# First layer of two 512-token chunks by seven block products (Strassen's scheme) in a last part of its own

## The chip, the cores and the metric

The kernel runs on one core of a Trainium2 chip. The metric is device time in microseconds (us) of one execution. Engines are named as in the profile: PE is TensorE (PEld its weight loads), DVE is VectorE, ACT is ScalarE, POOL is GpSimd, SP is SyncE, which here only issues loads.

## The reference

Four batches, 8 heads, 576 positions of 64 numbers go through an attention of two parts (one on means of four neighbours, one in a band of 7 positions); their sum is x, 2304 tokens of 512 numbers. Then follows a mixture of 8 experts in which every token goes through every expert:

```python
for e in range(E):                      # E = 8
    h = np.maximum(x @ w1[e], 0.0)      # [2304, 512] @ [512, 1024]
    ye = h @ w2[e]                      # [2304, 1024] @ [1024, 512]
    out += P[:, e:e + 1] * ye
```

P (2304 x 8) is the gate: exp of x @ w_gate, normalized by rows and columns in turn, eight times. It is known only when all of x is.

## The kernel before

The tokens are cut into chunks: 0, 1 and 5 have 256 tokens (small), 2, 3 and 4 have 512. F = 1024 is cut into eight blocks of 128, f = 0 to 7. Every fp32 operand is split into a high part in a 32-bit matmul type and a low part (operand minus high part), and a product is made of three matmuls: high by high, high by low, low by high.

A unit is one (expert, f): a w1 block and a w2 block of 256 KB each. `w_load` (L172, L175) loads them on SP's queue into the pool rawp, three units deep; `w_convert` has ACT copy the high part (L193) and POOL subtract the low part (L200; a few on DVE, L203). A step is one unit for one chunk. `mm1` (L957) makes h transposed: 4 blocks of the 512 inputs by 3 matmuls, 12 in all, with the weights stationary and up to 512 tokens moving, into a PSUM bank. ACT's relu gives the high part hh (L963), DVE's instruction from the bank and hh the low part hl (L966). `mm2` (L976 to L978) makes ye: 3 matmuls of 512 columns for each tile of 128 tokens, accumulated over the eight f. `mm1` of the next step stands ahead of `mm2` of this one.

Phase A runs while attention is still being computed. Its passes are in the list `order`: chunk 0 for e = 0 to 3, chunks 0 and 1 together for e = 4 to 7, then chunk 2, then chunk 3, for all e. There is no gate yet, so each pass's ye goes to DRAM (`spill`, L1145). Phase A ends at the first pass boundary behind which the gate is known. A planner with estimated costs (`pump`) mixes the attention's instructions in.

Phase B goes through the experts once; for each it takes chunk 3, chunk 4, chunk 1 (for e = 0 to 3) and chunk 5, so a unit is used by three or four steps. Units with f = 0 to 3 go to the pool wa, those with f = 4 to 7 to the pool wb, on the other (right) side of SBUF. `combine` (L1198, L1203) adds P times ye to the accumulator of a tile; `back_load` and `back_add` bring the spilled tiles back, up to three at a time, one add a step. Tiles that are complete go out by ACT's queue (L1209).

The order of instructions on each engine is that of the program.

## Time and profile before

| | |
|---|---|
| time, median of 3 | 1734.27 us (1733.5 to 1735.94) |
| profiled execution | 1733.57 us, span 1731.8 us |
| PE, PEld busy | 98%, 81% |
| DVE, ACT, POOL busy | 45%, 29%, 39% |
| PE clock granted, mean | 0.988 of full speed |
| DMA | 178.12 MB, mean 103 GB/s |

The span is the time from the first to the last instruction. Busy time is a share of the span; matmuls overlap, so PE's pace is read from the starts of its matmuls.

### The profile page before, as it was taken

What the parts mean: (1) busy time and instruction counts of PE and PEld (TensorE: products, weight loads), DVE (VectorE), ACT (ScalarE), POOL (GpSimd) and SP (SyncE); (2) the same over time, 40 slices, a digit from 0 to 9 for tenths busy, and PEclk for the clock granted to TensorE, in tenths of its full rate; (3) what the DMA queues carried; (4) which work ended last, traced back from release to release, by engine and by line L of the source; (5) the groups of instructions that cost most, each with busy time, mean ns of one, the idle gap of its engine ahead of it and who ended that gap; (6) DMA issues with size and microseconds to landing.
All of it is one profiled execution on the core that took longest, in us unless ns stands there. A gap on an engine that the chain in (4) does not pass through costs nothing.

```text
span 1731.8 us, 21860 instructions
## 1 busy us (share of the span) xinstructions
PE 1691.7 (98%) x8457; PEld 1405.0 (81%) x8457; DVE 787.0 (45%) x922; ACT 494.8 (29%) x1030; POOL 676.9 (39%) x479
## 2 busy tenths in 40 slices
PE   6988999999999999999999999999999999999998
PEld 4877888788788877888888888888888888888887
DVE  7678887798788784513433421121111111211112
ACT  1554443444344333331121131131131221311210
POOL 5889886587676554440040040040040220401300
PEclk7899999999999999999999999999999999999999
DMA  8786666677577533341251240030030120300101
GB/s 200 197 235 190 170 186 178 169 192 183 154 168 183 138 116 116 115 137 47 73 183 49 67 134 1 0 98 1 0 110 1 37 62 1 97 1 13 49 25 37
DMA packets 177609, 178.12 MB, mean 103 GB/s; under 512 B 10850, under 2 KB 127088, under 8 KB 177506
## 3 DMA queue, kind: packets, MB, share of 16 engines
q1 hardware_dynamic: 166754, 157.33, 34.2%
q10 hardware_dynamic: 10752, 19.40, 3.2%
q8 instruction: 66, 1.08, 0.3%
q14 instruction: 37, 0.30, 0.1%
HBM read 157.29 MB, written 19.40 MB: 102 GB/s over the span
## 4 chain that ended last, share of the span: by engine, by line
PE 78%; issue 10%; POOL 5%; DMA 5%; DVE 2%; ACT 0%; SPq 0%; POOLq 0%; ACTq 0%; DVEq 0%
PE psh L957 38%; PE psy L976 13%; PE psy L978 12%; PE psy L977 12%; DMA r<-in_moe_w_dram 3%; POOL w1l L200 2%; POOL w2l L200 2%; DVE lo L367 1%; POOL dr L449 1%; DMA dr<-in_k_dram 1%; DMA dr<-in_v_dram 1%; PE pss L673 0%; PE psg L808 0%; DMA lq<-in_q_dram 0%; PE psx L771 0%
## 5 line engine op out<-in xcount | busy, mean ns | idle before, releaser
L200 POOL TENSOR_TENSOR w1l<-r,w1h 128x512 fp32r<-128x512 f32 x192 | 280.3, 1460 | 867.6 <-ACT w1h L193 842.7
L966 DVE SCALAR_TENSOR_TENSOR hl<-psh,hh 128x512 fp32r<-128x512 f32 (+1 forms) x352 | 208.5, 592 | 851.7 <-ACT hh L963 851.6
L957 PE MATMUL psh<-xh,w1h 128*128 128x512 f32 (+1 forms) x1408 | 502.7, 357 | 2.7 <-ACT w1h L193 2.1
L957 PE MATMUL psh<-xl,w1h 128*128 128x512 f32 (+1 forms) x1408 | 497.6, 353 | 3.8 <-POOL xl L792 2.0
L957 PE MATMUL psh<-xh,w1l 128*128 128x512 f32 (+1 forms) x1408 | 497.4, 353 | 1.2 <-POOL w1l L200 1.2
L963 ACT ACTIVATE hh<-psh 128x512 fp32r<-128x512 f32 (+1 forms) x352 | 182.7, 519 | 981.2 <-PE psh L957 962.7
L976 PE MATMUL psy<-w2h,hh 128*128 128x512 f32 x1152 | 456.6, 396 | 0.1
L978 PE MATMUL psy<-w2h,hl 128*128 128x512 f32 x1152 | 451.8, 392 | 0.0
L977 PE MATMUL psy<-w2l,hh 128*128 128x512 f32 x1152 | 451.8, 392 | 0.0
L957 PEld LDWEIGHTS psh<-xh,w1h 128*128 128x128 f32 x1408 | 266.9, 190 | 47.0 <-ACT w1h L193 2.5
L957 PEld LDWEIGHTS psh<-xl,w1h 128*128 128x128 f32 x1408 | 267.2, 190 | 45.9 <-DVE xl L795 2.7
L957 PEld LDWEIGHTS psh<-xh,w1l 128*128 128x128 f32 x1408 | 267.1, 190 | 39.2 <-POOL w1l L200 1.8
L200 POOL TENSOR_TENSOR w2l<-r,w2h 128x512 fp32r<-128x512 f32 x183 | 272.5, 1489 | 42.5 <-ACT w2h L193 41.1
L978 PEld LDWEIGHTS psy<-w2h,hl 128*128 128x128 f32 x1152 | 216.4, 188 | 48.6 <-DVE hl L966 0.2
L976 PEld LDWEIGHTS psy<-w2h,hh 128*128 128x128 f32 x1152 | 216.9, 188 | 42.1 <-ACT hh L963 0.3
L977 PEld LDWEIGHTS psy<-w2l,hh 128*128 128x128 f32 x1152 | 216.8, 188 | 41.2
L193 ACT ACTIVATE w2h<-r 128x512 fp32r<-128x512 f32 x192 | 121.1, 630 | 166.1 <-POOL w1l L200 54.6
L367 DVE TENSOR_REDUCE lo<-prod 128x256 f32<-128x1792 f32 x36 | 123.8, 3441 | 0.3
L193 ACT ACTIVATE w1h<-r 128x512 fp32r<-128x512 f32 x192 | 120.1, 625 | 12.4 <-ACT sp L1144 6.0
L274 DVE TENSOR_TENSOR prod<-lq,lw 128x1792 f32<-128x1792 f32 x34 | 81.6, 2400 | 4.4 <-DMA lw<-in_k_dram 3.9
L336 DVE TENSOR_TENSOR prod<-lw,sc 128x1792 f32<-128x1792 f32 x33 | 79.4, 2405 | 0.6
L297 DVE TENSOR_REDUCE sc<-prod 128x28 f32<-128x1792 f32 x36 | 72.2, 2009 | 2.0 <-POOL prod L274 1.8
(121 smaller groups left out, 673.9 us busy)
## 6 DMA issues: line engine op xcount, KB each, us to landing
r<-in_moe_w_dram SPq DMA_DIRECT2D x384, 256.0 KB
spill<-sp ACTq DMA_DIRECT2D x56, 256.0 KB
s<-spill SPq DMA_DIRECT2D x56, 256.0 KB
dr<-in_k_dram SPq DMA_DIRECT2D x32, 144.0 KB
dr<-in_v_dram SPq DMA_DIRECT2D x32, 144.0 KB
dr<-in_q_dram SPq DMA_DIRECT2D x24, 144.0 KB
out_dram<-acc ACTq DMA_DIRECT2D x12, 256.0 KB
lw<-in_v_dram SPq DMA_DIRECT2D x4, 640.0 KB
```

Source lines behind the costliest of these rows:

```text
L193: nc.scalar.activation(out=h, in_=r, func=AF.Copy)
L200: nc.gpsimd.tensor_tensor(out=l, in0=r, in1=h.bitcast(F32), op=ALU.subtract)
L274: eng.tensor_tensor(out=pr[:, r0:r0 + nr], in0=with_free(qt[:, h, r0:], [(D, nr), (0, W), (1, D)]), in1=with_free(kt[:, h, r0:], [(D, nr), ...
L297: nc.vector.tensor_reduce(out=sc[:, h, r0:r0 + nr], in_=pr[:, r0:r0 + nr], axis=AX.X, op=ALU.add)
L336: eng.tensor_tensor(out=pr[:, r0:r0 + nr], in0=with_free(vt[:, h, r0:], [(D, nr), (D, W), (1, D)]), in1=with_free(sc[:, h, r0:], [(W, nr), ...
L367: nc.vector.tensor_reduce(out=ot[:, r0:r0 + nr, h % 2], in_=pr[:, r0:r0 + nr].rearrange("p r w d -> p r d w"), axis=AX.X, op=ALU.add,)
L957: nc.tensor.matmul(out=ps, lhsT=w[:, kk], rhs=x[:, kk], start=(i == 0), stop=(i == len(seq) - 1))
L963: nc.scalar.activation(out=hh, in_=ps, func=AF.Relu)
L966: nc.vector.scalar_tensor_tensor(out=hl, in0=ps, scalar=0.0, in1=hh.bitcast(F32), op0=ALU.max, op1=ALU.subtract)
L976: nc.tensor.matmul(out=y, lhsT=hh[:, ts], rhs=h2, start=(f == 0), stop=False)
L977: nc.tensor.matmul(out=y, lhsT=hh[:, ts], rhs=l2, start=False, stop=False)
L978: nc.tensor.matmul(out=y, lhsT=hl[:, ts], rhs=h2, start=False, stop=(f == NF - 1))
```

## The change

Chunks 3 and 4 leave the common passes. In front of them, everything else is finished: `order` now ends with chunks 1 and 5 together for e = 0 to 3 (their x lies side by side in the tiles xhs and xls) and chunk 5 for e = 4 to 7. There is one pass for one set of units there, so each step has a unit of its own, all in wa. In these steps two spilled tiles are added a step, and `t_gen` makes the four sums and differences T1 to T4 of the blocks of x of chunks 3 and 4 (high and low part), into the new pool cx.

The last part goes through experts and halves of F. A half has four f. `w1_gen` takes two raw blocks of w1 and makes high and low parts of A11, A12, A22 and of the sums S1 to S4 for a pair of f, into wb for the first pair and wa for the second; it runs during the second layer of the half before. `m_pair` makes h of two f and two chunks by seven products of 256 x 128 x 512 with six matmuls each, and puts them together in PSUM (two products are added onto a bank that has been read) and by ACT and DVE. The high and low parts of h of a whole half lie in tiles that earlier held x of the small chunks (chunk 3) and of chunk 2 (chunk 4). Then the second layer of the half follows for 8 tiles, with a `combine` for each tile and half.

Also, the pool su4 goes: the first chunk's `xs` and `qf` use the h buffers of the pool hp. Pool accp closes before the last part, and accumulators and intermediate tiles of the last part (accc, ct) take its place.

```diff
--- before.py
+++ after.py
+    smalls = [c for c in range(NC) if is_small(c)]
+    NS = R * chunks[0][1]
+    for nm in ("xhs", "xls"):
+        x01.append(xp.tile([128, KD, len(smalls) * NS], F32R, name=nm))
+    for i, c in enumerate(smalls):
+        xh[c], xl[c] = (x[:, :, i * NS:(i + 1) * NS] for x in x01)
...
-        xs = (ap2 if c else su4).tile([128, R, n], F32, tag="xs", name="xs")
+        pl, tg = (ap2, "xs") if c else (hp, ("hh", "hl")[p // 2])
+        xs = pl.tile([128, R, n], F32, tag=tg, name="xs")
...
-        qf = ini.tile([128, 2, 2, 2, Q0], F32, name="qf")
+        qf = hp.tile([128, 2, 2, 2, Q0], F32, tag="hl", name="qf")
         nc.vector.memset(qf, 0.0)
 
         n_small = 4
         order = [((0,), e) for e in range(n_small)] + [((0, 1), e) for e in range(n_small, E)]
-        order += [((c,), e) for c in (2, 3) for e in range(E)]
-        late = {}
+        order += [((2,), e) for e in range(E)]
+        order += [((1, NC - 1), e) for e in range(n_small)] + [((NC - 1,), e) for e in range(n_small, E)]
...
+        ca, cb = 3, 4
+        n_done = n // NF
+        rest = order[n_done:]
...
+        cx = ctx.enter_context(tc.tile_pool(name="cx", bufs=1, side="right"))
         wb = ctx.enter_context(tc.tile_pool(name="wb", bufs=4, side="right", reuse_waits="tile"))
+        th4 = cx.tile([128, 2 * KD, NS * 2], F32R, name="th4")
+        tl4 = cx.tile([128, 2 * KD, NS * 2], F32R, name="tl4")
+        few = ExitStack()
+        accp = few.enter_context(tc.tile_pool(name="accp", bufs=1, side="right", reuse_waits="tile"))
+        spr = few.enter_context(tc.tile_pool(name="spr", bufs=3, side="right", reuse_waits="tile"))
...
+        def t_gen():
+            for kk in range(2):
+                b11, b12, b21, b22 = (
+                    wb.tile([128, DM], F32R, tag="w1h" if kk == 0 else "w1l", name="bsum").bitcast(F32)
+                    for _ in range(4)
+                )
+                for b, c, k0 in ((b12, cb, 0), (b11, ca, 0), (b22, cb, 2), (b21, ca, 2)):
+                    nc.vector.tensor_tensor(
+                        out=b, in0=xh[c][:, k0 + kk].bitcast(F32), in1=xl[c][:, k0 + kk].bitcast(F32), op=ALU.add
+                    )
+                    yield
+
+                nc.vector.tensor_tensor(out=b11, in0=b12, in1=b11, op=ALU.subtract)
+                yield
+                nc.vector.tensor_tensor(out=b12, in0=b22, in1=b12, op=ALU.subtract)
+                yield
+                nc.vector.tensor_tensor(out=b22, in0=b22, in1=b11, op=ALU.subtract)
+                yield
+                nc.vector.tensor_tensor(out=b21, in0=b22, in1=b21, op=ALU.subtract)
...
+                for i, b in ((0, b11), (1, b22), (2, b12), (3, b21)):
+                    nc.scalar.activation(out=th4[:, 2 * i + kk], in_=b, func=AF.Copy)
+                    nc.vector.tensor_tensor(
+                        out=tl4[:, 2 * i + kk], in0=b, in1=th4[:, 2 * i + kk].bitcast(F32), op=ALU.subtract
+                    )
...
+        def w1_gen(pl, dst):
+            ra, rb = c_raw.pop(0), c_raw.pop(0)
+            hs = [pl.tile([128, KD, 128], F32R, tag="w1h", name="c1h") for _ in range(4)]
+            ls = [pl.tile([128, KD, 128], F32R, tag="w1l", name="c1l") for _ in range(4)]
+            dst.append((hs, ls))
+            top, bot = slice(0, 2), slice(2, 4)
+            def hi(i, r, s=slice(0, 4)):
+                nc.scalar.activation(out=hs[i][:, s], in_=r[:, s], func=AF.Copy)
+            def lo(i, r, s=slice(0, 4)):
+                nc.gpsimd.tensor_tensor(
+                    out=ls[i][:, s], in0=r[:, s], in1=hs[i][:, s].bitcast(F32), op=ALU.subtract
+                )
+            def tt(o, a, b, op):
+                nc.gpsimd.tensor_tensor(out=o, in0=a, in1=b, op=op)
+            hi(0, ra)
+            hi(1, rb, bot)
+            yield
+            lo(0, ra)
+            lo(1, rb, bot)
+            tt(rb[:, bot], rb[:, top], rb[:, bot], ALU.add)
+            tt(rb[:, top], ra[:, top], rb[:, top], ALU.subtract)
+            tt(ra[:, top], rb[:, bot], ra[:, top], ALU.subtract)
+            tt(ra[:, bot], ra[:, bot], ra[:, top], ALU.subtract)
+            yield
+            hi(2, ra)
+            hi(3, rb)
+            yield
+            lo(2, ra)
+            lo(3, rb)
+            for _ in range(2):
+                c_load()
+            yield
...
+        def w2_conv(f):
+            r = c_raw.pop(0)
+            h2 = wa.tile([128, DM], F32R, tag="w2h", name="w2h")
+            l2 = wa.tile([128, DM], F32R, tag="w2l", name="w2l")
+            nc.scalar.activation(out=h2, in_=r, func=AF.Copy)
+            nc.gpsimd.tensor_tensor(out=l2, in0=r, in1=h2.bitcast(F32), op=ALU.subtract)
+            w2_ops[f] = h2, l2
+            c_load()
...
+        for i, (piece, e) in enumerate(rest):
+            for f in range(NF):
+                steps.append((piece, e, f, n_a + i * NF + f))
...
+            while n_cv[0] < min(n + 5, len(units)):
                 w_convert(t2)
...
+                for _ in range(2):
+                    back_load()
+                    back_load()
+                    back_add()
+                next(tg, None)
+                next(tg, None)
+            if n_cv[0] >= len(units) and len(c_raw) >= 2:
+                if g0 is None:
+                    g0 = w1_gen(wb, wq)
+                next(g0, None)
...
+        few.close()
...
+        hh_of = {ca: x01[0][:, :, 0:512], cb: xh[2]}
+        hl_of = {ca: x01[1][:, :, 0:512], cb: xl[2]}
+        top, bot = slice(0, 2), slice(2, 4)
+        x_op = {
+            "B11": (xh[ca][:, top], xl[ca][:, top]),
+            "B21": (xh[ca][:, bot], xl[ca][:, bot]),
+            "B22": (xh[cb][:, bot], xl[cb][:, bot]),
+        }
+        for i in range(4):
+            s = slice(2 * i, 2 * i + 2)
+            x_op[f"T{i + 1}"] = th4[:, s], tl4[:, s]
+        w_op = {
+            "A11": (0, top), "A12": (0, bot), "A22": (1, bot),
+            "S2": (2, top), "S4": (2, bot), "S3": (3, top), "S1": (3, bot),
+        }
...
+        def bank():
+            pl, tag = ((ps_h, "h"), (ps_a, "a"))[bank_n[0] % 2]
+            bank_n[0] += 1
+            return pl.tile([128, DM], F32, tag=tag, name="psm")
+        def prod(ps, a, b, w, start=True):
+            i, s = w_op[a]
+            wh, wl = w[0][i][:, s], w[1][i][:, s]
+            bh, bl = x_op[b]
+            seq = [z for kk in range(2) for z in ((wh, bh, kk), (wh, bl, kk), (wl, bh, kk))]
+            for j, (wt, xt, kk) in enumerate(seq):
+                nc.tensor.matmul(
+                    out=ps, lhsT=wt[:, kk], rhs=xt[:, kk], start=start and j == 0, stop=j == len(seq) - 1,
+                    skip_group_check=not start,
+                )
+        def relu(c, f, t):
+            nc.scalar.activation(out=hh_of[c][:, f], in_=t, func=AF.Relu)
+        def relu_lo(c, f, t):
+            nc.vector.scalar_tensor_tensor(
+                out=hl_of[c][:, f], in0=t, scalar=0.0, in1=hh_of[c][:, f].bitcast(F32),
+                op0=ALU.max, op1=ALU.subtract,
+            )
...
+        def m_pair(w, f1, between):
+            f2 = f1 + 1
+            pa1 = bank()
+            prod(pa1, "A11", "B11", w)
+            s1 = ctile()
+            nc.scalar.activation(out=s1, in_=pa1, func=AF.Copy)
+            pb = bank()
+            prod(pb, "A12", "B21", w)
+            c11 = htile("hh")
+            nc.vector.tensor_tensor(out=c11, in0=pb, in1=s1, op=ALU.add)
+            relu(ca, f1, c11)
+            prod(pa1, "S2", "T2", w, start=False)
+            u2 = ctile()
+            nc.scalar.activation(out=u2, in_=pa1, func=AF.Copy)
+            relu_lo(ca, f1, c11)
+            between()
+            pd = bank()
+            prod(pd, "S3", "T3", w)
+            u3 = ctile()
+            nc.vector.tensor_tensor(out=u3, in0=pd, in1=u2, op=ALU.add)
+            pg = bank()
+            prod(pg, "S1", "T1", w)
+            c22 = htile("hl")
+            nc.vector.tensor_tensor(out=c22, in0=pg, in1=u3, op=ALU.add)
+            relu(cb, f2, c22)
+            relu_lo(cb, f2, c22)
+            ph = bank()
+            prod(ph, "A22", "T4", w)
+            c21 = htile("hh")
+            nc.vector.tensor_tensor(out=c21, in0=u3, in1=ph, op=ALU.subtract)
+            relu(ca, f2, c21)
+            relu_lo(ca, f2, c21)
+            between()
+            prod(pg, "S4", "B22", w, start=False)
+            c12 = htile("hl")
+            nc.vector.tensor_tensor(out=c12, in0=pg, in1=u2, op=ALU.add)
+            relu(cb, f1, c12)
+            relu_lo(cb, f1, c12)
+        def y_mm(y, c, t, f):
+            hh, hl = hh_of[c], hl_of[c]
+            h2, l2 = w2_ops[f]
+            ts = slice(t * 128, (t + 1) * 128)
+            nc.tensor.matmul(out=y, lhsT=hh[:, f, ts], rhs=h2, start=(f == 0), stop=False)
+            nc.tensor.matmul(out=y, lhsT=hh[:, f, ts], rhs=l2, start=False, stop=False)
+            nc.tensor.matmul(out=y, lhsT=hl[:, f, ts], rhs=h2, start=False, stop=(f == 3))
...
+                m_pair(wq[0], 0, between)
+                for g in gens:
+                    for _ in g:
+                        pass
+                m_pair(wq[1], 2, w2_next)
+                del wq[0:2]
+                for f in conv:
+                    w2_conv(f)
...
+                gens = []
+                if not last:
+                    gens = [w1_gen(wb, wq), w1_gen(wa, wq)]
+                def w1_next():
+                    for g in gens[:1]:
+                        if next(g, 0) == 0:
+                            del gens[0]
+                yt = [ps_y.tile([128, DM], F32, tag="y", name="psy") for _ in range(4)]
+                for f in range(2):
+                    for t in range(4):
+                        y_mm(yt[t], ca, t, f)
+                    w1_next()
+                for t in range(4):
+                    for f in range(2, 4):
+                        y_mm(yt[t], ca, t, f)
+                    combine(ca, t, e, yt[t], accc)
+                    w1_next()
+                for t in range(4):
+                    y = ps_y.tile([128, DM], F32, tag="y", name="psy")
+                    for f in range(4):
+                        y_mm(y, cb, t, f)
+                    combine(cb, t, e, y, accc)
+                    w1_next()
+                for g in list(gens):
+                    for _ in g:
+                        pass
```

## Rows read from the trace of the kernel before

**Rows 1.** Busy time of each engine by stage: the start and attention, the rest of the spilled passes, everything behind them, the end. Columns: the window, its length, then busy microseconds and count for each engine, the granted clock, the DMA share and GB/s.

```profile
0.00:250.00 250.00, 216.91 (x1309) 180.38 (x1310) 191.14 (x195) 107.94 (x261) 200.47 (x139) 0.92 0.77 199
250.00:747.77 497.77, 496.12 (x2350) 402.86 (x2349) 367.83 (x360) 202.93 (x421) 318.39 (x219) 1.00 0.58 154
747.77:1726.10 978.33, 978.26 (x4800) 821.73 (x4799) 226.81 (x367) 183.89 (x348) 158.06 (x122) 1.00 0.18 52
1726.10:1731.80 5.70, 0.40 (x2) 0.00 (x0) 1.18 (x2) 0.00 (x0) 0.00 (x0) 0.91 0.43 92
```

**Rows 2.** The chain that ended last, as shares of the span: by engine, and by line.

```profile
PE 78%; issue 10%; POOL 5%; DMA 5%; DVE 2%; ACT 0%; SPq 0%; POOLq 0%; ACTq 0%; DVEq 0%
PE psh L957 38%; PE psy L976 13%; PE psy L978 12%; PE psy L977 12%; DMA r<-in_moe_w_dram 3%; POOL w1l L200 2%; POOL w2l L200 2%; DVE lo L367 1%; POOL dr L449 1%; DMA dr<-in_k_dram 1%; DMA dr<-in_v_dram 1%; PE pss L673 0%; PE psg L808 0%; DMA lq<-in_q_dram 0%; PE psx L771 0%
```

**Rows 3.** The timeline of TensorE behind 747.77: the first first-layer matmul of a step with f = 2 and of the next step, of a step with f = 6 and of the next, of the step with f = 2 one pass later, and of two steps of chunk 1. Columns: start, duration, engine, line, operation, tiles, stationary and moving shape.

```profile
755.93 0.39 PE L957 MATMUL psh<-xh,w1h 128*128 128x512 f32 x1
...
761.37 0.39 PE L957 MATMUL psh<-xh,w1h 128*128 128x512 f32 x1
...
777.94 0.40 PE L957 MATMUL psh<-xh,w1h 128*128 128x512 f32 x1
...
783.53 0.40 PE L957 MATMUL psh<-xh,w1h 128*128 128x512 f32 x1
...
800.17 0.39 PE L957 MATMUL psh<-xh,w1h 128*128 128x512 f32 x1
...
843.25 0.28 PE L957 MATMUL psh<-xh,w1h 128*128 128x256 f32 x1
...
846.08 0.28 PE L957 MATMUL psh<-xh,w1h 128*128 128x256 f32 x1
```

**Rows 4.** The instructions that touch the DRAM tile spill: here the stores, with shortest, median and longest issue time in ns and first and last start in us.

```profile
L1145 ACTq DMA_DIRECT2D spill<-sp x56: 326/326/438, 79.9 to 749.6; - x56
```

**Rows 5.** The timeline around the end of a first-layer group, all engines: its last matmul, the next one, the relu, the low part. In square brackets the idle time before, and who ended it.

```profile
1442.82 0.39 PE L957 MATMUL psh<-xh,w1l 128*128 128x512 f32 x1
...
1443.05 0.39 PE L976 MATMUL psy<-w2h,hh 128*128 128x512 f32 x1
...
1443.24 0.60 ACT L963 ACTIVATE hh<-psh 128x512 fp32r<-128x512 f32 x1 [4.96 <-PE psh L957]
...
1443.87 0.69 DVE L966 SCALAR_TENSOR_TENSOR hl<-psh,hh 128x512 fp32r<-128x512 f32 x1 [2.24 <-ACT hh L963]
```

**Rows 6.** Instructions by line, whole run: shortest, median and longest duration in ns, first and last start in us. hh, hl, acc, w1h, w2l, s and r are in SBUF, psh and psy in PSUM.

```profile
L966 DVE SCALAR_TENSOR_TENSOR hl<-psh,hh x352: 408/690/700, 57.4 to 1724.2; 128x512 fp32r<-128x512 f32 x112, 128x256 fp32r<-128x256 f32 x64
...
L1203 DVE SCALAR_TENSOR_TENSOR acc<-psy,lg,acc x78: 739/742/751, 859.7 to 1726.5; 128x512 f32<-128x512 f32 x78
L1203 DVE SCALAR_TENSOR_TENSOR acc<-s,lg,acc x48: 740/743/1557, 787.8 to 1007.1; 128x512 f32<-128x512 f32 x48
...
L203 DVE TENSOR_TENSOR w2l<-r,w2h x9: 692/1341/1777, 56.4 to 178.9; 128x512 fp32r<-128x512 f32 x9
...
L193 ACT ACTIVATE w1h<-r x192: 613/624/635, 43.5 to 1617.4; 128x512 fp32r<-128x512 f32 x192
```

**Rows 7.** GpSimd: the two costliest groups of the page (busy us, mean ns, idle before and its releasers), then the same and the low part of x by line (shortest, median, longest ns).

```profile
L200 POOL TENSOR_TENSOR w1l<-r,w1h 128x512 fp32r<-128x512 f32 x192 | 280.3, 1460 | 867.6 <-ACT w1h L193 842.7
...
L200 POOL TENSOR_TENSOR w2l<-r,w2h 128x512 fp32r<-128x512 f32 x183 | 272.5, 1489 | 42.5 <-ACT w2h L193 41.1
...
L200 POOL TENSOR_TENSOR w1l<-r,w1h x192: 1266/1293/3534, 44.2 to 1618.1; 128x512 fp32r<-128x512 f32 x192
L200 POOL TENSOR_TENSOR w2l<-r,w2h x183: 1251/1296/3317, 45.5 to 1619.3; 128x512 fp32r<-128x512 f32 x183
...
L792 POOL TENSOR_TENSOR xl<-xs,xh x9: 722/737/2933, 52.0 to 663.1; 128x256 fp32r<-128x256 f32 x6, 128x512 fp32r<-128x512 f32 x3
```

**Rows 8.** Busy time in two windows in which the units of the second expert are loaded and converted beside steps of chunk 5 (columns as in rows 1).

```profile
859.00:885.00 26.00, 26.00 (x155) 22.98 (x154) 13.09 (x21) 12.76 (x25) 20.74 (x15) 1.00 0.73 221
862.00:882.00 20.00, 20.00 (x123) 17.82 (x123) 7.81 (x13) 10.45 (x21) 18.43 (x13) 1.00 0.78 232
```

**Rows 9.** The timeline of SyncE's DMA queue there: the issue of the w1 part of the first unit, and of the one seven units later (two w1 or w2 loads and some spilled tiles in between).

```profile
864.48 0.38 SPq L172 DMA_DIRECT2D r<-in_moe_w_dram  x1
...
885.34 0.38 SPq L172 DMA_DIRECT2D r<-in_moe_w_dram  x1
```

**Rows 10.** The timeline of the last microseconds: the last two accumulations, the last matmul, the output DMAs.

```profile
1725.83 1.45 DVE L1203 SCALAR_TENSOR_TENSOR acc<-psy,lg,acc 128x512 f32<-128x512 f32 x2 [1.25 <-PE psy L978]
...
1726.10 0.40 PE L978 MATMUL psy<-w2h,hl 128*128 128x512 f32 x1
1726.62 2.44 ACTq L1209 DMA_DIRECT2D out_dram<-acc  x4
```

**Rows 11.** The timeline of GpSimd from 862 us.

```profile
864.41 1.30 POOL L200 TENSOR_TENSOR w2l<-r,w2h 128x512 fp32r<-128x512 f32 x1
865.66 1.75 POOL L200 TENSOR_TENSOR w1l<-r,w1h 128x512 fp32r<-128x512 f32 x1
```

**Rows 12.** The timeline of VectorE from 862 us, the adds of spilled tiles.

```profile
862.55 0.74 DVE L1203 SCALAR_TENSOR_TENSOR acc<-s,lg,acc 128x512 f32<-128x512 f32 x1
...
870.21 1.08 DVE L1203 SCALAR_TENSOR_TENSOR acc<-s,lg,acc 128x512 f32<-128x512 f32 x1 [0.90 <-DMA s<-spill]
```

More of the change, by code (lines that the diff above doesn't have):

```diff
@@ L1172, in attention_moe_kernel @@
-        n_b = n
-        assert len(done_pairs) <= spill.shape[0]
-        if h_next is not None:
-            raise AssertionError
-        new = []
-        for rest, e in phase_b:
-            for f in range(NF):
-                new.append((e, f, (lambda: wa) if f % 8 < 4 else (lambda: late["wb"])))
-        assert all(units[n + i][:2] == new[i][:2] for i in range(n_dma[0] - n))
-        del units[n:]
-        units += new
-        wb = ctx.enter_context(tc.tile_pool(name="wb", bufs=4, side="right", reuse_waits="tile"))
@@ new lines, in attention_moe_kernel @@
+        while nb[1] < len(back):
+            back_load()
+            back_add()
+        while c_n[0] < 6:
+            c_load()
+        if g0 is None:
+            g0 = w1_gen(wb, wq)
+        for _ in g0:
+            pass
+        few.close()
+        accc = ctx.enter_context(tc.tile_pool(name="accc", bufs=1, side="right", reuse_waits="tile"))
+        ct = ctx.enter_context(tc.tile_pool(name="ct", bufs=4, side="right", reuse_waits="tile"))
+        hh_of = {ca: x01[0][:, :, 0:512], cb: xh[2]}
```

118 lines of the change are left out of this document (72 added, 46 removed).

## Prediction

> **What bounds the kernel now.** I read the windows by stage first. From 747.77 us, the first matmul behind the last spilled pass, to the last matmul at 1726.10, TensorE is busy 978.26 of 978.33 us at a granted clock of 1.00 [rows 1]. VectorE, ScalarE and GpSimd are busy 23%, 19% and 16% of it. The chain of waits says the same of the whole run: 78% is TensorE, 75 of it the two layers [rows 2]. So in this stretch the time is a count of matmuls times their spacing, and a saved matmul counts in full until another engine makes TensorE wait.
>
> The spacing comes from the starts in the timeline, not from the durations, which overlap. A step (24 matmuls of 512 columns) lasts 761.37 - 755.93 = 5.44 us, 0.2267 each, when its weights lie in pool wa; the steps f = 4 to 7 with weights in wb last 783.53 - 777.94 = 5.59, 0.233 each; a step of a small chunk (12 matmuls of 256 and 6 of 512 columns) lasts 846.08 - 843.25 = 2.83 [rows 3]; I use 2.82, since most of the others have that. Why wb is slower the trace does not say.
>
> **The change part by part.** All sums are against the profiled execution, 1733.57 us (span 1731.8 and 1.8 around it); the median of the runs is 0.7 above it.
>
> Phase A keeps its order up to the pass ((2,), e = 7): 56 spilled tiles are 4 x 2 + 4 x 4 + 8 x 4, exactly these passes [rows 4], so the new tail of `order` starts where phase A ends now. The move of `xs` and `qf` into pool hp touches only the time before the first matmul. I take 0, with 3 us either way.
>
> Strassen. Two chunks and two f cost 2 x 2 x 12 = 48 first-layer matmuls now and 7 x 6 = 42 then. There are 8 x 4 = 32 such groups: 192 matmuls less, 192 x 0.2267 = 43.5 us.
>
> Pairing chunk 1 with chunk 5 for four experts: 32 steps of 5.44 in place of 64 of 2.82, 6.4 us less.
>
> wa and wb. Now 16 passes of a large chunk have four slow steps each; from a step to the same step of the next pass are 800.17 - 755.93 = 44.24 against 8 x 5.44 = 43.52 us [rows 3], together 11.5. The new middle part uses wa alone. At the fast spacing the new stretch is 32 x 5.44 + 32 x 2.82 + 8 x 360 x 0.2267 = 174.1 + 90.2 + 652.9 = 917.2 us against 978.3 (61.1 less; the three terms make 61.4). In the last part, the weights of the first pair of each half lie in wb (672 matmuls) and the T sums in the new pool cx, on the same side (4 of 7 products of the second pair, 384 matmuls). If these run at 0.233, 1056 x 0.0062 = 6.6 us come back. Bounds: 0, and 2880 x 0.0062 = 18. I take 6.6, by the nearest rows.
>
> The ladder between ScalarE and VectorE. Today an h tile needs one ScalarE and one VectorE instruction in 5.44 us. In `m_pair` a group of 9.52 us has 9 on VectorE and 6 (with two w2 copies, 8) on ScalarE, in strict turns. Busy time is no issue: 9 x 0.7 = 6.3 and 5.0 us. The turns are. ScalarE starts 0.19 us behind the product's end (1443.24 against the next matmul's start at 1443.05), takes 0.60 from PSUM and 0.63 from SBUF, VectorE follows 0.03 later and takes 0.69 to 0.74 [rows 5, 6]. With products of 1.36 us, the fifth (S1 T1) ends at 6.80: c22 7.0 to 7.7, its relu to 8.3, relu_lo to 9.1, c21 to 9.7, relu to 10.4, relu_lo to 11.1, c12 to 11.7, relu to 12.4. Only then comes the next pair's copy `s1`, 12.4 to 13.0, because it stands behind that relu on ScalarE. TensorE wants to add S2 T2 into that bank at 9.52 + 2.72 = 12.24: it waits 0.8 us. The first pair of a half has no such ladder in front (s1 done at 2.2, needed at 2.7), the fourth use of a bank (c22 done 7.7, needed 8.2) holds, and the second layer hides the second pair's tail behind 24 matmuls of f = 0 and 1. 16 halves x 0.8 = 13 us. From below 0; from above with both relu_lo on the ladder slowed (second rival).
>
> Weights of the last part. GpSimd has 3 instructions of 128x512 and 5 of 128x256 a group, which I estimate at 3 x 1.29 + 5 x 0.74 = 7.6 us [rows 7], and 4 x 1.29 for w2 a half: 20.3 of 41.5 us (0.74 is a median of which six in nine have 256 columns). Both sets are made during the second layer, starting behind the last relu at about 22.4 and done near 40; the first is needed at 41.5. ScalarE's copies lie there too, where it has no relus. Loads are 4 MB per 83 us. All hidden: 0. The cover is 10 us for the first set.
>
> Middle part. In the steps of chunk 5 alone each 2.82 us needs a whole new unit, 0.5 MB. Now, between 864.48 and 885.34, seven units are loaded at 2.98 us each with the spilled tiles on the same queue, at 221 to 232 GB/s, and TensorE stays full [rows 8, 9]; without spills 186 GB/s are needed, and GpSimd's 2 x 1.29 = 2.58 fits. Behind a late transfer would wait the next load on SP's queue, then ScalarE's relu. Two back-adds a step instead of one, and the T sums (24 short VectorE groups), lie beside steps of 5.44 us with VectorE 23% busy. I take 0; above, 32 x 0.16 = 5 less five units of lead, so 4.
>
> Where the last part starts, the second weight set is made inside the first pair (GpSimd near 16 us, wanted near 13 to 15), and the new tiles lie where accumulators still being written out were: 3 us, between 0 and 8. The end: one output DMA of a full tile instead of four issues of 2.44 us in all [rows 10]: 1 less.
>
> Sum: 917.2 + 6.6 + 13 + 3 = 939.8, 38.5 less than 978.3, and 1 at the end: 1733.57 - 39.5 = 1694.1, beside the median 1695.
>
> **A page that speaks against it.** relu_lo reads PSUM and SBUF now, and is 0.69 whatever GpSimd does; then it reads two SBUF operands. An add of that kind (acc<-s) has a median of 743 and a maximum of 1557 ns, and w2l on VectorE 1341 in the stretch where GpSimd was busy [rows 6]; at 862 to 872 GpSimd's instructions beside such adds grow from 1.30 to 1.75, and the adds from 0.74 to 1.08 [rows 11, 12]. The Trainium skill (SBUF — State Buffer, "SBUF: two separate sides") says that VectorE instructions with two SBUF inputs and GpSimd's take the shared port pair as a lock for a whole instruction, the other one blocking. By that rule the ladder would lose a whole GpSimd instruction at each relu_lo (second rival). The trace agrees that they hinder each other, but the largest growth of an add, 1557 - 743 = 814 ns, is less than a whole one.
>
> **The rivals.**
> 1. TensorE never waits in the last part, because the ladder is shorter than I sum it: 1695 - 13 = 1682. For it: TensorE idles 0.07 us in this stretch today [rows 1]. Against: the ladder has nine turns and TensorE's margin is six products. 0.15.
> 2. The two relu_lo on the ladder meet GpSimd. At 1.34 instead of 0.74 each, 16 x 1.2 = 19: 1714; at 1.557, 26: 1721. Against it: the w2 copies reach GpSimd at 5.6 and 11.0 in the pair, between the relu_lo's places at 4.3, 8.4 and 10.4. 0.22. If each waits out a whole GpSimd instruction of 1.29 us [rows 7], 16 x 2 x 1.29 = 41: 1736, no change, 0.04.
> 3. Slower: the weight sets come late. The first set has 7.6 us of GpSimd work in a gap of 19; the gain of 39.5 is 2.5 us a half, so this decides from 21.6 us, a mean of 3.6 us per 128x512 instruction. Singles of 3.5 stand in the trace, the means are 1.46 and 1.49 [rows 7]. At 4 us the set takes 23.6, 4.6 late: 16 x 4.6 = 74, 1769. 0.04.
>
> **How the numbers follow.** The forecast has 0.55, with its own range 1686 to 1705 (slow spacing between 0 and 18, 3 us at either seam). The range for 8 in 10 takes in the first rival and most of the second: 1677 to 1720. A difference below 0.2% (3.5 us) is no change here. Faster 0.93, same 0.03, slower 0.04.
>
> **What would show it.** Phase A's end near 748; the middle part near 264 us; eight experts of some 84 us each; TensorE's only waits in the last part 16 times near 0.8 us, at the second pair's S2 T2, behind ScalarE's copy s1. An expert near 81.6 shows rival 1; relu_lo above 1 us and waits near 2 rival 2; waits for c1l behind GpSimd at the start of a half rival 3. I am wrong if TensorE waits at the start of the second layer, or if phase A moves.

## The result, and the profile after

The changed kernel takes 1695.38 us, median of 4 runs (1693.8 to 1696.94); the kernel before took 1734.16 beside it (1733.5 to 1735.94). The ratio is 0.9775, 95% interval 0.9758 to 0.9792: 38.8 us faster. The forecast was 1695. That agreement is partly luck: the middle part came out 3.4 us longer than its term and phase A ended 1.65 later, while the last part was 3.2 shorter and the end behind it 0.5.

All numbers below are of the profiled execution, 1695.34 us, with a span of 1693.6. Its windows by stage, with the columns of [rows 1]: the middle part and the last part. Phase A ends at 749.42, the last matmul starts at 1689.38.

```profile
749.42:1017.13 267.71, 265.23 (x1346) 226.06 (x1345) 121.08 (x167) 108.46 (x200) 169.07 (x130) 1.00 0.61 187
1017.13:1689.38 672.25, 662.96 (x2881) 539.14 (x2879) 290.48 (x417) 211.93 (x380) 315.03 (x313) 1.00 0.17 52
```

The stretch behind phase A is 267.71 + 672.25 = 939.96 us, where it was 978.33. TensorE was busy all but 0.07 us of it before [rows 1]; now it idles 2.5 us in the middle part (267.71 - 265.23) and 9.3 in the last one. VectorE and GpSimd have gone from 23% and 16% of this stretch to 44% and 51%, DMA from 0.18 to 0.61 in the middle part. The engines that feed TensorE have less room, and where that matters the view of the waits says by whom (TensorE's waits from 749.42 to 1689.38; columns: who waits and for whom, us in total, times, longest):

```profile
PE psm L1400 <- ACT cs L1426: 8.0, 17, 1.3
PE psy L980 <- ACT hh L967: 1.4, 2, 1.0
PE psm L1400 <- POOL c1l L1283: 1.3, 1, 1.3
PE psy L982 <- DVE hl L970: 1.1, 1, 1.1
```

Line 1426 is the copy `s1`; 16 halves have 17 such waits, one in each second pair, and one in the very first pair. The chain that ended last agrees only in part:

```profile
PE 68%; POOL 13%; issue 9%; DVE 5%; ACT 2%; DMA 2%; SPq 0%; POOLq 0%; ACTq 0%; DVEq 0%
```

TensorE has fallen from 78% to 68% [rows 2] and GpSimd risen from 5 to 13, yet behind phase A TensorE waits for GpSimd once, for 1.3 us. The chain steps back to whatever released an instruction, even where that had been done in good time; for the price of a wait the view of the waits is the better one.

The first matmul of four halves of the last part (start, duration, engine, line, operation, tiles, shapes):

```profile
1017.13 0.39 PE L1400 MATMUL psm<-xh,c1h 128*128 128x512 f32 x1
1062.28 0.39 PE L1400 MATMUL psm<-xh,c1h 128*128 128x512 f32 x1
...
1229.57 0.39 PE L1400 MATMUL psm<-xh,c1h 128*128 128x512 f32 x1
1271.39 0.39 PE L1400 MATMUL psm<-xh,c1h 128*128 128x512 f32 x1
```

The first half takes 45.15 us, every other one 41.82. A half has 180 matmuls, 40.81 at 0.2267. Of the 1.01 us more, 0.68 stand at one place, S2 T2 of the second pair: from the matmul before it to its first one are 0.79 to 0.80, and from there to the next 0.34, against 0.2267 each. The other 0.34 are spacing of 0.230 to 0.234 in part of the products. So the last part is 16 x 40.81 = 652.9, 16 x 0.68 = 10.9 of waits at `s1`, 16 x 0.34 = 5.4 of slow spacing, and 45.15 - 41.82 = 3.3 for the first half; the sum, 672.5, is one spacing more than the 672.25 to the start of the last matmul.

One ladder, from the second half of a first pair (ScalarE and VectorE; in brackets the idle time before and who ended it; the h tiles lie where x tiles were and go by their names, xh and xhs for the high, xl and xls for the low parts):

```profile
1236.64 0.69 DVE L1444 TENSOR_TENSOR cc<-psm,cs 128x512 f32<-128x512 f32 x1 [0.60 <-PE psm L1400]
1237.37 0.63 ACT L1406 ACTIVATE xh<-cc 128x512 fp32r<-128x512 f32 x1 [2.27 <-DVE cc L1444]
1238.04 0.69 DVE L1409 SCALAR_TENSOR_TENSOR xl<-cc,xh 128x512 fp32r<-128x512 f32 x1 [0.70 <-ACT xh L1406]
1238.64 0.68 DVE L1450 TENSOR_TENSOR cc<-cs,psm 128x512 f32<-128x512 f32 x1
1239.36 0.63 ACT L1406 ACTIVATE xhs<-cc 128x512 fp32r<-128x512 f32 x1 [1.36 <-DVE cc L1450]
1240.02 0.69 DVE L1409 SCALAR_TENSOR_TENSOR xls<-cc,xhs 128x512 fp32r<-128x512 f32 x1 [0.70 <-ACT xhs L1406]
1240.63 0.68 DVE L1456 TENSOR_TENSOR cc<-psm,cs 128x512 f32<-128x512 f32 x1
1241.35 0.63 ACT L1406 ACTIVATE xh<-cc 128x512 fp32r<-128x512 f32 x1 [0.84 <-DVE cc L1456]
1241.89 0.58 ACT L1426 ACTIVATE cs<-psm 128x512 f32<-128x512 f32 x1
```

This is c22, its relu and low part, c21, its relu and low part, c12 and its relu, in strict turns. The pair began at 1229.57, so c22 starts at 7.07, c21 at 9.07, c12 at 11.06 (forecast 7.0, 9.1 and 11.1). The last row is `s1` of the second pair, behind the relu of c12 on ScalarE; it ends at 1242.47, and TensorE's S2 T2, which adds into the bank that it reads, starts at 1242.52.

### The profile page after: what moved, and what is told of

Read it like the earlier page. It is cut to its first block, busy times and chain, and to the rows that moved or that the text cites. A ratio compares the mean times of both kernels' runs of the same rounds, so it can differ in the third digit from the quotient of the medians.

```text
span 1693.6 us, 21978 instructions
## 1 busy us (share of the span) xinstructions
PE 1646.8 (97%) x7881; PEld 1352.1 (80%) x7881; DVE 972.9 (57%) x1138; ACT 630.6 (37%) x1262; POOL 1002.8 (59%) x799
## 4 chain that ended last, share of the span: by engine, by line
PE 68%; POOL 13%; issue 9%; DVE 5%; ACT 2%; DMA 2%; SPq 0%; POOLq 0%; ACTq 0%; DVEq 0%
PE psh L961 15%; PE psm L1400 13%; PE psy L1466 7%; PE psy L1465 7%; PE psy L1464 7%; POOL w2l L203 6%; POOL w1l L203 5%; PE psy L980 5%; PE psy L982 5%; PE psy L981 5%; PE psv L527 1%; DVE lo L370 1%; DMA dr<-in_v_dram 1%; DVE cc L1444 1%; DVE xls L1409 1%
## 5 line engine op out<-in xcount | busy, mean ns | idle before, releaser
L980 PE MATMUL psy<-w2h,hh 128*128 128x512 f32 x640 | 255.8, 400 | 1.4 <-ACT hh L967 1.4
L982 PE MATMUL psy<-w2h,hl 128*128 128x512 f32 x640 | 250.3, 391 | 1.1 <-DVE hl L970 1.1
L981 PE MATMUL psy<-w2l,hh 128*128 128x512 f32 x640 | 250.6, 392 | 0.0
L1193 DVE SCALAR_TENSOR_TENSOR acc<-psy,lg,acc 128x512 f32<-128x512 f32 x140 | 103.9, 750 | 199.3 <-PE psy L1466 198.7
L961 PE MATMUL psh<-xhs,w1h 128*128 128x256 f32 (+1 forms) x512 | 176.7, 345 | 2.8 <-ACT w1h L196 2.1
L961 PE MATMUL psh<-xls,w1h 128*128 128x256 f32 (+1 forms) x512 | 174.6, 341 | 3.8 <-POOL xls L796 2.0
L961 PE MATMUL psh<-xhs,w1l 128*128 128x256 f32 (+1 forms) x512 | 174.1, 340 | 1.0 <-POOL w1l L203 1.0
L1283 POOL TENSOR_TENSOR c1l<-r,c1h 128x512 fp32r<-128x512 f32 (+1 forms) x128 | 145.0, 1159 | 36.9 <-ACT c1h L1280 36.9
L982 PEld LDWEIGHTS psy<-w2h,hl 128*128 128x128 f32 x640 | 120.5, 188 | 27.7 <-DVE hl L970 1.8
L961 PEld LDWEIGHTS psh<-xls,w1h 128*128 128x128 f32 x512 | 98.2, 192 | 16.9 <-DVE xls L799 2.7
L961 PEld LDWEIGHTS psh<-xhs,w1h 128*128 128x128 f32 x512 | 98.0, 191 | 17.0 <-ACT w1h L196 2.5
```

What stands on the lines that cost most here:

```text
L961: nc.tensor.matmul(out=ps, lhsT=w[:, kk], rhs=x[:, kk], start=(i == 0), stop=(i == len(seq) - 1))
L980: nc.tensor.matmul(out=y, lhsT=hh[:, ts], rhs=h2, start=(f == 0), stop=False)
L981: nc.tensor.matmul(out=y, lhsT=hh[:, ts], rhs=l2, start=False, stop=False)
L982: nc.tensor.matmul(out=y, lhsT=hl[:, ts], rhs=h2, start=False, stop=(f == NF - 1))
L1283: nc.gpsimd.tensor_tensor(out=ls[i][:, s], in0=r[:, s], in1=hs[i][:, s].bitcast(F32), op=ALU.subtract)
```

## The experiments

My theory: the change saves 43.5 us of matmuls by the seven products and 17.9 by pairing and the use of wa; about 11 of that go to the wait for `s1`, because the copy is queued behind the relu of c12; about 5 go to slow spacing; the rest of what is lost are single waits in the middle part and where the last part starts. Rivals: the low parts are slowed by GpSimd's use of SBUF (rival 2 of the prediction); the ladder as a whole is too slow, so that taking one wait away only moves it; the slow spacing belongs to the far side of the memory.

**The new order without the seven products.** The last part keeps its place and the large chunks' order, but does its first layer by eight block products, with the relu straight from PSUM.

```diff
 def m_pair(w, f1, between):
-    prod(pa1, "A11", "B11", w)
...
+    for g in range(2):
+        for c in (ca, cb):
...
+                seq += [(hs[g], xh[c], kk), (hs[g], xl[c], kk), (ls[g], xh[c], kk)]
...
+            nc.scalar.activation(out=hh_of[c][:, f], in_=ps, func=AF.Relu)
```

> The last part as after, but its first layer by eight block products (48 matmuls a group, relu straight from PSUM, no sums of weights; the T sums are still made, unused). If the gain is matmuls that are left out, less a wait of 0.68 us a half: a half goes from 41.82 us to 192 x 0.2267 = 43.5, and some 0.3 for the slow spacing, 16 halves are 27 to 32 us longer, span 1719 to 1726. If the gain came from the small chunks and the pools: span within 10 us of 1693.6.

Measured: 1722.76 us (1721.47 to 1727.78), ratio 0.9939 (0.9917 to 0.9961). The middle part takes 267.3 us, each half 43.85, and TensorE is busy in all of it:

```profile
1063.00:1690.00 627.00, 627.00 (x2746) 515.37 (x2745) 164.95 (x229) 129.01 (x231) 144.79 (x114) 1.00 0.16 47
```

What follows: order, pairing and the use of wa give 10.5 us of the gain (span 1721.3 against 1731.8), the seven products the other 27.7. The 10.5 are less than the 17.9 of pairing and wa, since this middle part has 3.0 us of waits (267.3 against 264.3) and this last part 5.3 of slow spacing (16 x 0.33, a half being 192 x 0.2267 = 43.52 without it). By the terms: the last part is 701.32 here and 672.25 with the products, 29.1 less; 43.5 of matmuls, less 10.9 for `s1`, less 3.3 at the seam (the longer first half), less 0.3 more slow spacing is 29.0. The wait and the seam exist only with the seven products.

**`s1` ahead of the last relu.** The first product of the second pair and its copy are issued before the relu of c12. Nothing else is changed.

```diff
+        def m_head(w):
+            pa1 = bank()
+            prod(pa1, "A11", "B11", w)
+            s1 = ctile()
+            nc.scalar.activation(out=s1, in_=pa1, func=AF.Copy)
+            return pa1, s1
...
+            h2 = nxt() if nxt is not None else None
             relu(cb, f1, c12)
             relu_lo(cb, f1, c12)
```

> Only the place of one ScalarE instruction changes: the second pair's copy s1 stands ahead of the relu of c12. If the wait at the second pair's S2 T2 is made by ScalarE's order: the wait (0.56 us and a slow matmul behind it) goes in all 16 halves, a half lasts 41.1 to 41.2, span 1681 to 1685. If the ladder as a whole is too long and the wait only moves (to a bank that c12 or c22 still reads): halves of 41.6 or more, span 1689 to 1694.

Measured: 1685.14 us (1682.67 to 1688.53), ratio 0.9717 (0.9699 to 0.9735), 10.2 us less than the changed kernel. A half takes 41.16 (1266.31 - 1225.15). ScalarE in that half, then TensorE's waits of the whole last part:

```profile
1236.44 0.60 ACT L1424 ACTIVATE cs<-psm 128x512 f32<-128x512 f32 x1 [0.34 <-PE psm L1400]
1236.94 0.63 ACT L1406 ACTIVATE xh<-cc 128x512 fp32r<-128x512 f32 x1
```

```profile
PE psm L1400 <- POOL c1l L1283: 1.8, 1, 1.8
PE psm L1400 <- ACT cs L1424: 1.3, 1, 1.3
```

The copy (line 1424) now waits for its product alone, comes before the last relu, and ends at 1237.04, half a microsecond before S2 T2 starts at 1237.54. The 16 waits are gone; what is left lies in the first half, which takes as long as before (45.17). The turns of the ladder themselves are as long as before (from the start of c22 to that of c12 3.99 us, 1232.23 to 1236.22, as in the changed kernel), so the rival that the ladder as a whole is too slow falls: one place in ScalarE's order was the cost.

**GpSimd kept busy beside the ladder.** Five more subtractions of 128x512 fp32 on GpSimd in each pair, whose result nobody uses.

```diff
+        def dummy(n):
+            for _ in range(n):
+                nc.gpsimd.tensor_tensor(
+                    out=dumt, in0=th4[:, 0].bitcast(F32), in1=tl4[:, 0].bitcast(F32), op=ALU.subtract
+                )
...
             nc.scalar.activation(out=s1, in_=pa1, func=AF.Copy)
+            dummy(3)
...
             relu_lo(cb, f2, c22)
+            dummy(2)
```

> Five more GpSimd subtractions of 128x512 in each m_pair (their result is not used), so that GpSimd is busy for some 9 of 10 us there. If relu_lo with two SBUF operands and GpSimd hinder each other (second rival of the prediction): relu_lo 1.0 to 2.0 us in place of 0.69, the wait at S2 T2 grows to 1.2 to 3.2 us, halves of 42.5 to 44.4, span 1705 to 1735. If they don't: relu_lo 0.69 and halves of 41.8.

Measured: 1711.32 us in one run; a half takes 42.78 in the mean, 0.96 more. VectorE and GpSimd at the same place of the ladder, then the instruction of line 1411 in all the last part (shortest, median, longest ns):

```profile
1243.48 1.59 DVE L1411 SCALAR_TENSOR_TENSOR xl<-cc,xh 128x512 fp32r<-128x512 f32 x1 [0.70 <-ACT xh L1408]
...
1248.35 1.63 DVE L1411 SCALAR_TENSOR_TENSOR xl<-cc,xh 128x512 fp32r<-128x512 f32 x1 [0.70 <-ACT xh L1408]
...
1241.86 2.66 POOL L1424 TENSOR_TENSOR dumt<-th,tl 128x512 f32<-128x512 f32 x2
...
1248.16 1.27 POOL L1424 TENSOR_TENSOR dumt<-th,tl 128x512 f32<-128x512 f32 x1
```

```profile
L1411 DVE SCALAR_TENSOR_TENSOR xls<-cc,xhs x64: 691/693/1782, 1023.7 to 1685.1; 128x512 fp32r<-128x512 f32 x64
L1411 DVE SCALAR_TENSOR_TENSOR xl<-cc,xh x64: 691/1566/1660, 1028.2 to 1687.1; 128x512 fp32r<-128x512 f32 x64
```

The low part that starts at 1243.48 ends at 1245.07, 0.55 behind the end of GpSimd's work at 1244.52; the one at 1248.35 ends at 1249.98, 0.55 behind 1249.43. So it does not run slowly beside GpSimd, it waits out the instruction that is running. The whole last part of this run agrees: 69 of its 128 low parts start while a GpSimd instruction runs, and each ends 0.54 to 0.55 behind that one, between 0.73 and 1.78 us after its own start; the other 59 take 0.69. That is what the Trainium skill says (SBUF — State Buffer, "SBUF: two separate sides": of a VectorE instruction with two SBUF inputs and a GpSimd one that reads SBUF, whoever starts first holds the shared ports for its whole instruction, and the other blocks); these runs agree. In the prediction I held against that rule that no add had grown by a whole GpSimd instruction: that was a wrong reading, since the one that loses pays only what is left of it.

In the changed kernel the same instruction is at its 693:

```profile
L1409 DVE SCALAR_TENSOR_TENSOR xls<-cc,xhs x64: 693/693/1625, 1022.7 to 1668.6; 128x512 fp32r<-128x512 f32 x64
L1409 DVE SCALAR_TENSOR_TENSOR xl<-cc,xh x64: 691/693/1344, 1027.2 to 1670.6; 128x512 fp32r<-128x512 f32 x64
```

All that are longer than 0.75 (four) stand in the first half, where GpSimd makes a weight set beside the ladder. Rival 2 is a real mechanism that the placing of GpSimd's work avoids in 15 of 16 halves.

**The pairing undone.** Chunks 1 and 5 go as two steps of 256 tokens per unit for the four experts, in place of one of 512.

```diff
             for f in range(NF):
-                steps.append((piece, e, f, n_a + i * NF + f))
+                for p in piece:
+                    steps.append(((p,), e, f, n_a + i * NF + f, p == piece[-1]))
```

> Chunks 1 and 5 as two steps of 256 tokens on the same unit for e = 0 to 3, all else as after. If pairing saves by spacing and number of matmuls: 32 x (2 x 2.82 - 5.44) = 6.4 us longer in the middle part (267.7 to 274), the last part unchanged, span near 1700. If pairing gives nothing on the chip: below 2 us.

Measured: 1715.71 us in one run, the middle part 287.9: a miss, since 274 was expected. TensorE's waits there, and two windows around the largest:

```profile
PE psy L980 <- ACT hh L967: 5.5, 6, 1.9
PE psy L982 <- DVE hl L970: 5.0, 3, 4.5
```

```profile
783.30:788.20 4.90, 0.40 (x2) 0.00 (x0) 2.93 (x6) 0.87 (x2) 1.26 (x1) 0.86 0.78 237
788.20:793.60 5.40, 5.37 (x19) 4.79 (x20) 3.12 (x6) 1.01 (x2) 1.28 (x1) 0.50 0.18 34
```

VectorE's low part stood behind adds that waited for spilled tiles (VectorE was idle for 6.44 us until such a tile had come, at 784.91, and came to the low part at 787.76). TensorE ran two matmuls in 4.9 us, and then the granted clock was 0.50, its lower level of 1.2 GHz, for 5.4 us, with matmuls of 512 columns 0.43 apart; behind it, 1.00 again. So I tried the same with better pacing:

```diff
-                for _ in range(2):
-                    back_load()
-                    back_load()
+                back_load()
+                back_load()
+                if si >= 12:
...
```

> As the unpaired run, but spilled tiles are added one a unit, two units later than their loads, so that relu_lo never stands behind an add that waits for a load. If pairing itself is worth 6.4 us and the rest of the 20 us of the unpaired run came from that queue: middle part 272 to 275 us, no wait for hl above 0.5 us. If the 256-column steps wait for another reason: 280 or more.

Measured: 1709.79 us in one run, the middle part 280.5: not the first case but just the second. The pacing did what it was meant to for the low part (TensorE's longest wait for it is 0.3 us), but 9.5 us go to waits and what follows them, most for relus: in the longest, 3.1 us, the relu stood on ScalarE behind an output DMA that waited for VectorE's add (until 1027.1) and two conversions of weights that waited for GpSimd (until 1027.7). Without its waits the part takes 271.0, and that of the changed kernel without its own (3.2) 264.5. The step count of pairing is thus worth 6.5 us, as forecast; the rest of the difference, 6.3, are waits. Why there are more of them is my reading and no run tests it alone: work on an engine beside TensorE has 2.8 us to hide in with a short step and 5.44 with a paired one. That second value of the pairing is not in my sum.

**Byte places of the tiles.** In the built program the tiles of x, of h and of the weights on the left side of SBUF begin at 1728 modulo 2048 bytes of a partition, those of the right side (the T sums, the first pair's weights, and pool wb of the kernel before) at 2016. 1728 is a multiple of 64, 2016 is not. 288 bytes left free on the right side make it 1728 there too.

```diff
+        padp = ctx.enter_context(tc.tile_pool(name="padp", bufs=1, side="right"))
+        pad = padp.tile([128, 72], F32, name="pad")
+        nc.gpsimd.memset(pad, 0.0)
```

> 288 bytes a partition are left free behind the right end, so that wb, cx and all on the right side begin at the same place within 2 KB as the tiles on the left (1728 in place of 2016 bytes behind a multiple of 2048). If the slow spacing (0.233 for 0.2267) comes from that difference: the first layer of a half gets up to 0.3 us shorter, a half 41.5, span 5 us less. If it comes from the distance of the two operands or from other traffic: 41.82 as after.

Measured: 1692.94 us in one run. A half takes 41.57, and but for a few behind each wait all matmuls are 0.2267 apart. Of the 0.34 of slow spacing a half gets back 0.25, mainly because TensorE, being earlier, waits 0.07 longer for `s1` (0.86 between the two starts, 0.79 before). It is still not 16 x 0.25 = 4 us faster, because its first half takes 46.63: behind the three waits there, 1.76, 1.00 and 1.68 us to the next start, matmuls run 0.43 apart for some 3 us. A window there:

```profile
1034.50:1037.50 3.00, 3.00 (x9) 2.33 (x8) 1.07 (x1) 1.12 (x2) 1.22 (x2) 0.50 0.59 175
```

The granted clock is 0.50 of full speed in it, its lower level of 1.2 GHz. The changed kernel has the same three waits (1.68, 1.00, 1.69) and no such stretch; which of the two happens, these runs do not tell.

The run also leaves open whether the multiple of 64 counts or the same place within 2 KB as the other operand. With 32 bytes free (`[128, 8]` in place of `[128, 72]`) the right side begins at 1984, a multiple of 64 at another place.

> The changed kernel with 32 bytes a partition left free on the right side instead of 288, so that the tiles of the right side begin at multiples of 64 bytes (1984 modulo 2048), but at another place within 2 KB than those of the left side (1728). If the slow spacing of the second pair comes from tiles that do not begin at a multiple of 64 bytes: all products at 0.2267 us a matmul, a half of the last part at 41.5 us as with 288 bytes, the span near 1690. If it comes from two operands at different places within 2 KB: 0.233 stays in the second pair, a half of 41.8, the span near 1694.

Measured: 1690.64 us in one run, a half 41.56 (1269.20 - 1227.64). The T products of the second pair, six matmuls from row to row, in the changed kernel and in this one:

```profile
1245.42 0.39 PE L1400 MATMUL psm<-th,c1h 128*128 128x512 f32 x1
...
1246.82 0.39 PE L1400 MATMUL psm<-th,c1h 128*128 128x512 f32 x1
```

```profile
1243.36 0.39 PE L1403 MATMUL psm<-th,c1h 128*128 128x512 f32 x1
...
1244.72 0.39 PE L1403 MATMUL psm<-th,c1h 128*128 128x512 f32 x1
```

1.40 us against 1.36, 0.2333 against 0.2267. So the place within 2 KB does not matter: an operand at 1984 beside one at 1728 is as fast as two at 1728. Two readings are left: an operand that begins off a multiple of 64 bytes is slow by itself, or two operands that begin at different places within 64 bytes are slow together. The changed kernel speaks for the second. The T products of the first pair have both operands at 2016, and twelve matmuls of them take 2.72 us from row to row, 0.2267 each:

```profile
1233.72 0.39 PE L1400 MATMUL psm<-th,c1h 128*128 128x512 f32 x1
...
1236.44 0.39 PE L1400 MATMUL psm<-th,c1h 128*128 128x512 f32 x1
```

No run moves the left side and leaves the right one, so this is not tested further. If the byte at which the tiles begin is what made wb slow, the kernel before must gain by the same three lines ahead of its pool wb:

> The kernel before with 288 bytes a partition left free on the right side, so that its right-hand weight sets begin at 1728 modulo 2048, as the left-hand ones do, instead of 2016. If the place of the tile in its bytes is what made its steps of f = 4 to 7 take 5.59 us against 5.44: every step of the middle and of the last part takes 5.44, 0.14 to 0.15 less in some 80 steps, 11.5 us in all, 1722 to 1724 us. If it is the far side of the memory: no change, 1734.

Measured: 1722.94 us (1720.9 to 1724.22), ratio 0.9926 (0.9909 to 0.9943) beside 1735.72 for the kernel before. The first first-layer matmul of three steps that follow one another, of fourteen equal ones in a row:

```profile
773.49 0.39 PE L957 MATMUL psh<-xh,w1h 128*128 128x512 f32 x1
...
778.93 0.39 PE L957 MATMUL psh<-xh,w1h 128*128 128x512 f32 x1
...
784.37 0.39 PE L957 MATMUL psh<-xh,w1h 128*128 128x512 f32 x1
```

All of the large chunks' steps are 5.44 us, with wb too, where [rows 3] had 5.59. The side of the memory is not the cause, and 12.8 us can be had in the kernel before without any of the change. The Trainium skill (SBUF — State Buffer, "Operand start alignment") asks only that an operand begins at a multiple of its element size, and says that the runs behind it timed nothing. Here 2016 is a multiple of 4, and beside an operand at 1728 it costs 3% of a matmul's spacing (0.2333 against 0.2267).

Neither reading explains that in the changed kernel A11 B11 and S4 B22 of the second pair, whose operands both lie on the left side, run at 0.230 to 0.232 (with 32 or 288 bytes free: 0.2267).

**The small chunks' output on SyncE's queue.**

```diff
-                    nc.scalar.dma_start(out=dst, in_=a[p0:p0 + m])
+                    (nc.sync if is_small(c) else nc.scalar).dma_start(out=dst, in_=a[p0:p0 + m])
```

> Output DMAs of the small chunks are issued on SP's queue and not on ScalarE's. If their issues (0.6 us each in the rows) hold ScalarE's copies and relus: the waits at the change to chunk 5 alone (1.05 us) and at the first S2 T2 of the last part (1.45 us) go, span 1690 to 1692. If the loads behind them on SP's queue then come late: new waits for w1h or w2h in the middle part, 268 us or more.

In the changed kernel ScalarE comes to the first `s1` only behind four output issues and two conversions; with the output on SyncE's queue it is there at once:

```profile
1017.41 2.44 ACTq L1199 DMA_DIRECT2D out_dram<-acc  x4
1019.90 0.93 ACT L1280 ACTIVATE c1h<-r 128x512 fp32r<-128x512 f32 x2 [4.33 <-issue]
1020.74 0.58 ACT L1426 ACTIVATE cs<-psm 128x512 f32<-128x512 f32 x1
```

```profile
1017.73 0.60 ACT L1426 ACTIVATE cs<-psm 128x512 f32<-128x512 f32 x1 [2.32 <-PE psm L1400]
```

Measured: 1694.04 us in one run, half a hit. The first wait of the last part is gone, but its first half still takes 45.02: eight matmuls about 0.43 apart behind the wait for GpSimd's c1l took the gain back:

```profile
1031.50:1034.50 3.00, 3.00 (x8) 2.33 (x8) 1.44 (x1) 1.11 (x2) 0.94 (x2) 0.50 0.62 184
```

The granted clock is 0.50 here. The wait near 930 us stayed, since there ScalarE's relu stands behind two output issues of chunk 2, a large one, which wait for VectorE's adds. ScalarE in this run:

```profile
928.99 1.24 ACTq L1199 DMA_DIRECT2D out_dram<-acc  x2
930.33 0.38 ACT L967 ACTIVATE hh<-psh 128x256 fp32r<-128x256 f32 x1 [4.08 <-DVE acc L1193]
```

**What helped, together.** `s1` ahead, the small chunks' output on SyncE, the 288 bytes, and three spilled tiles loaded one step earlier:

```diff
+            if 1 <= si < 4:
+                back_load()
```

> The copy s1 ahead, the small chunks' outputs on SP's queue, the place within 2 KB, and three loads of spilled tiles ahead of the first add. If the waits seen in the traces add up: 10.9 + 2.5 + 1.2 us less than after, and 0 to 5 for the spacing: span 1674 to 1680. If they hide one another: span 1681 to 1685, as with s1 ahead alone.

Measured: 1678.71 us (1676.68 to 1680.1), ratio 0.9678 (0.9662 to 0.9695), 16.7 us below the changed kernel. From the second half on TensorE does not wait:

```profile
1063.00:1660.00 597.00, 597.00 (x2635) 494.37 (x2634) 265.58 (x384) 194.95 (x351) 286.23 (x284) 1.00 0.17 50
```

A half is 40.80 (1262.69 - 1221.89), which is 180 x 0.2267: all that this count of matmuls takes at that spacing. The wait near 788 us is gone; the runs with one of the other three edits alone still have it (gaps of 1.44 us), so the early loads took it away. Left are 2.5 us in the first half (waiting for c1l) and two waits of some 0.8 us in the middle part.

## Why the prediction was right, point by point

**Phase A, 0 with 3 either way.** It ended at 749.42 in place of 747.77. The ten kernels with the new order, in which phase A is the same, ended it between 747.31 and 751.41, so 1.65 can't be told from scatter.

**The count of matmuls.** 43.5 us for the 192 matmuls, 6.4 for pairing and 11.5 for the use of wa in the middle part all hold: the last part without waits and slow spacing is 652.9, the middle part without its waits 264.5 against 264.3, and the kernel before with 288 bytes free shows the 11.5 alone (1722.94 against 1735.72, its steps 5.44).

**Slow spacing, 6.6.** 5.4, and the size was right for a wrong reason. I gave it to pool wb and its side of the memory, and counted the matmuls that touch that side. What counts is the byte at which the two operands' tiles begin. My count was also wrong in its parts: T with the first pair's weights is fast, two left-side products are slow.

**The ladder, 13.** 10.9. The mechanism is as forecast: 16 waits, at S2 T2 of the second pair, behind `s1`, which stands behind the relu of c12. The step that was mis-sized is the wait itself, 0.8 a half: the gap between the two starts is 0.8, but 0.23 of it is the ordinary spacing, and 0.11 more are lost between the next two: 0.68.

**Seam, 3.** 3.3 was measured, by another way. I named late weights and tiles still being written out. The weights were one part (GpSimd's c1l, a gap of 1.69). The other was ScalarE's order: four output issues of 0.61 us each and two conversions ahead of the first `s1`, a gap of 1.68. In my sum ScalarE's issuing of the small chunks' output stands nowhere.

**The middle part, 264.3 with waits of 0 to 4.** 267.71. The 3.2 us of waits are three places. The largest, a gap of 1.45 us between two starts near 788, is VectorE's queue:

```profile
784.96 0.49 DVE L1188 TENSOR_SCALAR acc<-s,lg 128x512 f32<-128x512 f32 x1 [6.81 <-DMA s<-spill]
786.35 0.97 DVE L1188 TENSOR_SCALAR acc<-s,lg 128x512 f32<-128x512 f32 x1 [0.91 <-DMA s<-spill]
787.24 1.28 DVE L1227 TENSOR_TENSOR bsum<-xh,xl 128x512 f32<-128x512 f32 x2
788.44 0.68 DVE L970 SCALAR_TENSOR_TENSOR hl<-psh,hh 128x512 fp32r<-128x512 f32 x1
```

VectorE stood 6.81 us at an add whose spilled tile had not come, and the low part of h, which TensorE needed, was queued behind it, a second add and two of the T sums. I had taken 0 because VectorE was 23% busy: the average share hid a head-of-queue wait. The other two are ScalarE's relu behind output issues, and behind conversions that waited for GpSimd.

**The weights of the last part, 0.** Held. GpSimd's instructions had the durations that I estimated (1294 and 740 ns in the mean), and in the half from 1229.57 it is done with both sets at 1269.99, before the next half at 1271.39. Only in the first half is there no second layer of its own to make them beside.

**The end, 1 less.** From the start of the last matmul to the end of the span are 4.2 us (1693.6 - 1689.38), where they were 5.7: 1.5 less.

**The rivals.** The first (no wait, 1682) is what the kernel becomes with `s1` moved (1685.14 measured): the rest of the ladder fits. In the changed kernel itself it did not occur. The second is a mechanism of the chip, shown by the busy GpSimd; in this kernel it touches the first half alone. The third did not occur.

## What to carry to other kernels

When an exact saving of matmuls puts new work on the side engines, look for the first instruction of the next group that stands behind the last one of this group in an engine's order: here a copy that needed nothing from the ladder cost 10 us by its place alone, with ScalarE below 40% busy. Price output DMAs as instructions of the engine that issues them, and adds of loaded tiles as waits at the head of their queue. If the spacing of equal matmuls differs between pools, look at the byte at which the tiles of both operands begin: 32 or 288 bytes left free took 4 us of slow spacing away here (16 x 0.25), and 288 took 12.8 us off the kernel before.

## What was not expected of the hardware

Matmuls of 512 fp32r columns (the 32-bit matmul type) were 0.2333 us apart with one operand's tile beginning at 2016 and the other's at 1728 modulo 2048 bytes of a partition, and 0.2267 with 1984 and 1728, with both at 1728 (but for two products of the changed kernel), and with both at 2016. A VectorE instruction with two SBUF operands blocked until the running GpSimd instruction, which read SBUF too, had ended, and finished 0.55 us behind it, where it takes 0.69 alone. After TensorE had stood still for most of 4.9 us the granted clock was 0.50 for 5.4 us, and behind a wait of 3.1 us (the unpaired one with better pacing) for some 3. In the first half of three runs (the first unpaired one, the one with 288 bytes free, the one with the output on SyncE) it was 0.50 for some 3 us behind a wait of 1.7 us that followed others; there, in the changed kernel and the runs with 32 bytes free, with `s1` ahead, with GpSimd kept busy and with what helped together, it stayed at 1.00 behind waits of 1.7 to 2.7 us. Where it fell behind a wait of 1.7 us, matmuls 0.43 apart cost about as much again as the wait. Behind the single waits of 0.8 us of the other halves it stayed at 1.00.
